# V asked for two batches at a time, fewer weight pieces with places of their own, and new places in the order of work

## The chip, the cores and the metric

One Trainium2 chip; the kernel runs on one of its cores. The metric is the device time of one execution in microseconds. Lower is better.

## The reference

Two stages. The first is causal attention with B = 8 batches, H = 8 heads, S = 576 positions, D = 64, and Nb = 16 beacon positions ahead of the keys that every query sees. The second is a soft mixture of experts over the N = 4608 tokens that come out, with E = 8 experts of 4 slots each, Dm = 512 and F = 1024. All inputs are float32.

```python
k_all = np.concatenate([beacon_k, k], axis=2); v_all = np.concatenate([beacon_v, v], axis=2)
scores = where(causal, -1e9, q @ k_all.T / sqrt(D))
a = softmax(scores);  x = (a @ v_all) as (B*S, H*D)
logits = x @ phi                                  # (N, 32)
d = softmax(logits, over tokens);  slot_input = d.T @ x
for e in range(E): slot_out[e] = relu(slot_input[e] @ w1[e]) @ w2[e]
out = softmax(logits, over slots) @ slot_out      # (4608, 512) float32
```

## The kernel before

**Steps.** The attention runs in 32 steps, one for each pair of heads; `n` is the step, `divmod(n, 4)` gives the batch `b` and the pair `g` in it. In a step the scores of pair `n` are made in four parts (letters `0` to `3`; each ends in an exponential on ScalarE, and part 1 is followed by two masking operations on GpSimd, L339), and the products with V of pair `n - 1` are made (`A` and `B`), then normalised on VectorE (`N`). Two pairs make a quad of q and of k; `T` and `U` transpose the next quad's halves. `x` takes one piece of the second stage's work on the previous batch from a list (`Q` fills it).

**Order.** The whole order of a step is a string of letters in the table `order`: the entry at minus `n` if there is one, else that of `n % 4`. All engines work through their own instructions in the order in which the letters issue them, so a letter's place decides what waits behind what on each engine.

**V.** V of one batch comes as two tiles of 128 partitions by 8 heads by two rows of 64 (`load_v`, tag `vf`, 512 KB a request, three buffers) and a tail of 80 rows (`load_tail`, tag `vl`). The letters a, b, e, f (first tile) and g, h, i, j (second tile) each cast a quarter of a tile from float32 to float16 into `vh[b % 2]`, on GpSimd or, for those in the string `dve`, on VectorE. `t` casts the tail, `c` and `d` load the beacons' V. At `g = 0` these letters mean the batch that just runs, else the next one, so `f` and `i` of a batch are done in its own first step.

**Requests on SyncE (SP).** V, tails, and q and k of the quads (`load_quad`, four requests of 288 KB, three buffers each) are requested from SP's queue, in the order in which `requests(n)` after each step writes them. SP goes through its queue on its own; a request whose buffer is still read waits there, and all behind it wait too.

**Weights.** The experts' weights are 32 pieces of 1 MB in float32, written as float16 by requests from GpSimd's queue (`load_w`). Letter `w` asks for pieces until `want(n)` are requested; in step 31 the rest is. 24 pieces have places of their own (12 tiles of 8 KB a partition in the pool `wh`, which the output tiles take over at the end); the last eight take buffers of V, q and k (`homes`). The last three pieces (`halved`) come in two halves of columns, all first halves ahead of all second halves.

**End.** After step 31 come the last routing pieces, `layer1` with ReLU, `turn` (transposes into `hTz`, a tile that GpSimd has to clear first, L654), `layer2` over the pieces in order, and the output rows, first for the left half of three groups, then their right half, then six whole groups of 1 MB.

Of the kernel before, what the change touches and what calls it, by code (L numbers as in the profile page):

```python
# [8 lines left out]
FP = mybir.dt.float32  # L9
F16 = mybir.dt.float16  # L10
# [7 lines left out]
def kernel(  # L18
# [22 lines left out]
    UL = U - 4 * P  # L41
# [12 lines left out]
    GB = H // 2  # L54
# [21 lines left out]
    qkp = ctx.enter_context(tc.tile_pool(name="qkp", bufs=3))  # L76
    vfp = ctx.enter_context(tc.tile_pool(name="vfp", bufs=3))
    vlp = ctx.enter_context(tc.tile_pool(name="vlp", bufs=2))
    exq = ctx.enter_context(tc.tile_pool(name="exq", bufs=2))
    sml = ctx.enter_context(tc.tile_pool(name="sml", bufs=4))  # L80
    NW = 24
    wh = ctx.enter_context(tc.tile_pool(name="wh", bufs=NW // 2))
    sc_scope = ExitStack()
    ps_sc = sc_scope.enter_context(tc.tile_pool(name="ps_sc", bufs=1, space=PSUM, side="right"))
# [3 lines left out]
    qf, kf = {}, {}  # L88
# [18 lines left out]
                    in_=src[b, h0:h0 + 2].rearrange("h s d -> (h s) d").rearrange(  # L107
                        "(p j) d -> p j d", j=J))

    vf = {}  # L110
    vten = v.tensor

    def vpairs(row, n, step, h0=0, nh=H):
        return bass.AP(vten, (row + h0 * S) * D, [[step * D, n], [S * D, nh], [1, step * D]])

    def load_v(b, what):
        base = b * H * S - Nb
        if what in (0, 1):
            t = vf[(b, what)] = vfp.tile([P, H, 2 * D], FP, name="vf", tag="vf")
            if what == 0 and b == 0:  # L120
                nc.vector.memset(t[0:Nb // 2, 0:1, :], 0.0)
                nc.sync.dma_start(out=t[Nb // 2:P, 0:1, :], in_=vpairs(base + Nb, P - Nb // 2, 2, 0, 1))
                nc.sync.dma_start(out=t[:, 1:H, :], in_=vpairs(base, P, 2, 1, H - 1))
            else:
                nc.sync.dma_start(out=t[:, :, :], in_=vpairs(base + 2 * P * what, P, 2))

    def load_tail(b):
        vf[(b, 2)] = vlp.tile([P, H, D], FP, name="vl", tag="vl")
        (nc.sync if b else nc.gpsimd).dma_start(
            out=vf[(b, 2)][0:UL], in_=vpairs(b * H * S - Nb + 4 * P, UL, 1))  # L130

    def put_t(b, eng):
        eng.tensor_copy(out=vh[b % 2][0:UL, 4, :, 0:D], in_=vf[(b, 2)][0:UL])

    def load_beac(b, r):
        nc.gpsimd.dma_start(out=vh[b % 2][64 * r:64 * r + Nb // 2, 0, :, 0:D],
# [1 line left out]

    NPC = 4 * E
    wv = {}  # L140
    homes = ["vf", "vf", "qf", "kf", "vf", "qf", "kf", "qf", "kf"][:NPC - NW]
    assert len(homes) == NPC - NW

    XH = 3
# [5 lines left out]
    def load_w(x):  # L150
        (e, r), hf = reqs[x]
        m = pieces.index((e, r))
        if (e, r) not in wv:
            if m < NW:
                if m % 2 == 0:
                    wv["pair"] = wh.tile([P, 4096], F16, name="w", tag="w")
                t = wv["pair"][:, 2048 * (m % 2):2048 * (m % 2) + 2048]
            else:
                tag = homes[m - NW]
                pool, cols = {"vf": (vfp, 2048), "qf": (qkp, 2304), "kf": (qkp, 2304)}[tag]  # L160
                t = pool.tile([P, cols], F16, name="wx", tag=tag)[:, 0:2048]
            wv[(e, r)] = t
        t = wv[(e, r)]
        if r < 2:
            src = moe_w1[e, r * 256:r * 256 + 256].rearrange("(s p) f -> p s f", p=P)
            t = t.rearrange("p (s f) -> p s f", s=2)
        else:
            src = moe_w2[e, (r - 2) * 512:(r - 1) * 512].rearrange("(p s) d -> p s d", p=P)
            if hf is None:
                src = src.rearrange("p s d -> p (s d)")  # L170
            else:
                src = src[:, :, 256 * hf:256 * hf + 256]
                t = t.rearrange("p (s d) -> p s d", s=4)[:, :, 256 * hf:256 * hf + 256]
        nc.gpsimd.dma_start(out=t, in_=src)  # L174
# [16 lines left out]
    bv0 = setup[0:Nb // 2, 1024:2048].rearrange("p (h x) -> p h x", h=H)  # L191
    nc.gpsimd.dma_start(out=bv0, in_=beacon_v[0].rearrange("h (n r) d -> n h (r d)", r=2))
    load_first(1)
    load_v(0, 0)
    load_v(0, 1)
    load_quad(1)
    load_quad(2)
    phif = const.tile([P, NDC, NSL], FP, name="phif")
# [29 lines left out]
    vh = [const.tile([P, NCH, H, DD], F16, name=f"vh{i}") for i in range(2)]  # L228
# [11 lines left out]
    hTz = const.tile([P, NFC, E * HY], F16, name="hTz")  # L240
# [31 lines left out]
    def beac(m):  # L272
        nc.gpsimd.tensor_copy(out=kT[m % 2][:, :, 0:Nb], in_=bkT[:, 2 * m:2 * m + 2, :])
# [111 lines left out]

    def put_v(b, R, z, r, eng):
        eng.tensor_copy(out=vh[b % 2][64 * r:64 * r + 64, 2 * R + z, :, 0:D],  # L387
                        in_=vf[(b, R)][64 * z:64 * z + 64, :, D * r:D * r + D])

    def put_b(r, eng):  # L390
        eng.tensor_copy(out=vh[0][64 * r:64 * r + Nb // 2, 0, :, 0:D],
# [125 lines left out]
    wl = 0  # L517

    def want(n):
        return int(0.64 * n) if n < 24 else int(15 + 2 * (n - 24))  # L520

    lastb = [lambda: xt_last(0, nc.vector), lambda: xt_last(1, nc.vector), lambda: sums(0, 6)]
    casts = {"a": (0, 0, 0), "b": (0, 0, 1), "e": (0, 1, 0), "f": (0, 1, 1),
             "g": (1, 0, 0), "h": (1, 1, 1), "i": (1, 0, 1), "j": (1, 1, 0)}
    dve = "fej"
    order = {0: "0Awf1xB2kNxi3TU", 1: "01QxbA2Ba3NTwU", 2: "0h1tAxckdx2BwxN3TU", 3: "01AjxBNg23eTwU",
             -2: "0ABwaT1ZV2NWiUbk3", -3: "01AcB2dN3weTU", -4: "0A1htBfgNj2kwp3TU", -5: "01baAwBNQ2x3TU",
             -29: "0QAB1N2xxx3w", -30: "0xABN1x2xw3L", -31: "0Ax1B2Nwxx3x"}

    def step(n, c):  # L530
        nonlocal wl
        b, g = divmod(n, GB)
        vb = b if g == 0 else b + 1
        if c in "0123":
            score(n, int(c))
        elif c == "A":
            for a in range(2):
                attend(n - 1, a, (0, 1, 2))
        elif c == "B":
            for a in range(2):  # L540
                attend(n - 1, a, (3, 4))
        elif c == "N":
            norm(n - 1)
        elif c == "x":
            if work:
                work.pop(0)()
        elif c == "Q":
            work.extend(routing(b - 1))
        elif c == "L":
            work.extend(lastb)  # L550
        elif c in "TUVW":
            m, w = (n // 2 + 1, 1) if n % 2 == 0 else ((n + 3) // 2, 0)
            if n == 1:
                m, w = 1, int(c in "VW")
            elif c in "VW":
                w = 0
            if m < NQ:
                transp(m, w, int(c in "UW"), n == 1 and c in "UW")
        elif c in "abefghij":
            if vb < B:  # L560
                put_v(vb, *casts[c], nc.vector if c in dve else nc.gpsimd)
        elif c in "cd":
            if vb < B:
                load_beac(vb, "cd".index(c))
        elif c == "t":
            if vb < B:
                put_t(vb, nc.vector if c in dve else nc.gpsimd)
        elif c == "Z":
            beacons()
        elif c == "p":  # L570
            nc.gpsimd.tensor_copy(out=phih[:, :, :, :],
                                  in_=phif[:, :, :].unsqueeze(2).broadcast_to([P, NDC, 4, NSL]))
        elif c == "k":
            if n // 2 + 1 < NQ:
                beac(n // 2 + 1)
        elif c == "w":
# [6 lines left out]
    def next_quad():  # L583
        if quads:
            load_quad(quads.pop(0))

    early = "0r1qq"
    reqs_at = {0: "1q", 1: "", 2: "r0q", 3: "", -2: "0r"}

    def requests(n):  # L590
        b, g = divmod(n, GB)
        for c in reqs_at.get(-n, reqs_at[g]):
            if c == "1" and b + 1 < B:
                load_v(b + 1, 1)
            elif c == "0" and b + 2 < B:
                load_v(b + 2, 0)
            elif c == "q":
                next_quad()
            elif c == "r" and b + 2 < B:
                load_tail(b + 2)  # L600

    score(0, 0)
    score(0, 1)
# [8 lines left out]
    for r in range(2):  # L612
# [4 lines left out]
        out=bkf[:, :, :],  # L617
        in_=beacon_k.rearrange("b h n d -> (b h n) d").rearrange("(p j) d -> p j d", j=8))
    nc.gpsimd.dma_start(out=phif[:, :, :], in_=moe_phi.rearrange("(c p) e -> p c e", p=P))
    score(0, 3)  # L620
    for c in early:
        if c in "01":
            load_v(1, int(c))
        elif c == "r":
            load_tail(1)
        else:
            next_quad()
    for x in range(4):
        score(1, x)
    for c in "TUABNVW":  # L630
        step(1, c)
# [19 lines left out]
    si_piece(B - 1)  # L651
    logit_piece(B - 1, 1)
    assert wl == len(reqs)
    nc.gpsimd.memset(hTz[:, :, :], 0.0)  # L654
# [135 lines left out]
```

## Time and profile before

| | |
|---|---|
| three runs | 206.95, 208.53, 209.72 us; median 208.53 |
| profiled execution | 206.11 us, of which the profile's span is 204.4 us |
| mean granted TensorE clock | 0.959 |
| busy: PE, VectorE, ScalarE, GpSimd | 157.4, 129.7, 131.3, 111.8 us |
| moved by DMA | 55.81 MB in 46217 packets, mean 273 GB/s |
| weights | 24 requests into own places, 11 into borrowed ones |
| V | 16 requests of about 512 KB, 8 tails of 160 KB |

Times are microseconds from the first instruction of the profiled execution. The three runs lie within 1.3% of one another. A busy share is an average over stages with different limits; DMA rates count the bytes as they are written, so a weight that is read as float32 and written as float16 counts half of what is read.

### The profile page before, as it was taken

How to read it: one execution, taken by the hardware profiler on the slowest of the kernel's cores; microseconds unless marked ns; L12 is line 12 of the kernel's file. 1: busy time of each engine (PE TensorE's matmuls, PEld its weight loads, DVE VectorE, ACT ScalarE, POOL GpSimd, SP SyncE). 2: the span in 40 equal slices, each digit the busy share in tenths (PEclk: the TensorE clock that was granted, in tenths of full speed). 3: DMA queues.
4: the chain of work that ended last, by engine and by line, in shares of the span. 5: the costliest groups of instructions: out<-in, count | busy, mean ns of one | idle time of the engine just before them, and what ended most of it. 6: DMA issues, size and time to landing. Idle time of an engine off the chain costs nothing.

```text
span 204.4 us, 7928 instructions
## 1 busy us (share of the span) xinstructions
PE 157.4 (77%) x3474; PEld 115.4 (56%) x3474; DVE 129.7 (63%) x270; ACT 131.3 (64%) x195; POOL 111.8 (55%) x194
## 2 busy tenths in 40 slices
PE   0777884999987889987879889899889867878300
PEld 0646662677765657765557667677668535643100
DVE  2594876578776777866686778679725320679500
ACT  2584787289876687876687778688685320389400
POOL 8394379757559657746853794899556341000000
PEclk9999999699999999999999999999999996999955
DMA  6999999998999999999999999999999999999996
GB/s 202 305 353 303 275 396 252 293 245 257 189 346 295 245 336 264 266 196 345 311 233 344 274 265 199 315 193 188 213 212 215 215 209 198 151 331 370 422 417 285
DMA packets 46217, 55.81 MB, mean 273 GB/s; under 512 B 8791, under 2 KB 31311, under 8 KB 45415
## 3 DMA queue, kind: packets, MB, share of 16 engines
q1 hardware_dynamic: 34391, 37.55, 57.6%
q0 software_dynamic: 11648, 17.46, 47.8%
q8 instruction: 27, 0.44, 0.8%
q10 hardware_dynamic: 144, 0.29, 0.5%
q14 instruction: 7, 0.06, 0.1%
HBM read 62.75 MB, written 9.44 MB: 353 GB/s over the span
## 4 chain that ended last, share of the span: by engine, by line
PE 35%; POOL 19%; DMA 12%; issue 12%; ACT 7%; DVE 6%; POOLq 1%; DVEq 0%; ACTq 0%
PE av L368 10%; PE sc L315 9%; POOL ex L339 8%; DMA wx<-in_moe_w_dram 7%; ACT ex L327 5%; PE tr L285 4%; POOL vh L387 4%; DVE osb L710 4%; POOL w L174 3%; DMA vh<-in_beacon_v_dram 3%; PE tr L410 3%; DMA setup<-in_beacon_k_dram 3%; PE av L691 2%; ACT osb L708 2%; PE tr L425 2%
## 5 line engine op out<-in xcount | busy, mean ns | idle before, releaser
L327 ACT ACTIVATE ex<-sc 128x1024 f16<-128x1024 f32 (+3 forms) x128 | 105.4, 869 | 33.7 <-PE sc L315 21.2
L339 POOL TENSOR_SCALAR_AFFINE_SELECT ex<-ex 64x512 f16<-64x512 f16 x64 | 40.6, 634 | 38.4 <-ACT ex L327 36.6
L315 PE MATMUL sc<-qT,kT 64*64 64x80 bf16 (+4 forms) x768 | 47.0, 304 | 6.3 <-ACT ex L327 3.7
L368 PE MATMUL av<-vh,ex 128*128 128x65 f16 x945 | 42.9, 199 | 6.0 <-DMA vh<-in_beacon_v_dram 2.8
L368 PEld LDWEIGHTS <-ex 128*128 128x128 f16 (+1 forms) x960 | 37.1, 107 | 15.8 <-issue 7.6
L315 PEld LDWEIGHTS <-kT 64*64 64x64 bf16 x768 | 20.8, 108 | 17.9 <-issue 9.9
L387 POOL CAST vh<-vf 64x512 f16<-64x512 f32 x37 | 23.4, 635 | 11.4 <-DMA vf<-in_v_dram 9.7
L382 DVE TENSOR_TENSOR xb<-av,r 128x640 f16<-128x640 f32 (+1 forms) x32 | 26.1, 814 | 1.1
L286 DVE COPY kT<-tr 128x640 bf16<-128x640 bf16 (+1 forms) x29 | 21.3, 773 | 4.7 <-PE tr L285 4.1
L286 DVE COPY qT<-tr 128x640 bf16<-128x640 bf16 (+1 forms) x29 | 21.3, 765 | 1.6 <-PE tr L285 1.4
L379 DVE RECIPROCAL r<-av 128x10 f32<-128x10 f32 (+1 forms) x32 | 7.0, 218 | 22.5 <-PE av L368 22.5
L708 ACT ACTIVATE osb<-fp,rc 128x256 f32<-128x256 f32 (+1 forms) x24 | 12.8, 578 | 11.6 <-PE fp L706 11.0
L174 POOL DMA_DIRECT2D w<-in_moe_w_dram x24 | 16.2, 677 | 0.0
L323 PE MATMUL sc<-mk,idb 64*64 64x128 bf16 x256 | 15.5, 223 | 0.6 <-issue 0.6
L387 DVE CAST vh<-vf 64x512 f16<-64x512 f32 x27 | 15.1, 558 | 0.7
L285 PE MATMUL tr<-idb,qf 128*64 128x128 bf16 x270 | 12.4, 235 | 3.7 <-issue 2.8
L710 DVE TENSOR_SCALAR osb<-fp,rc 128x256 f32<-128x256 f32 (+1 forms) x24 | 13.6, 614 | 2.0 <-PE fp L706 1.9
L706 PE MATMUL fp<-soh,eLh 128*128 128x256 f16 (+1 forms) x48 | 11.6, 324 | 3.1 <-ACT osb L708 1.5
L415 DVE COPY xT<-tr 128x1024 f16<-128x1024 f16 x14 | 9.6, 691 | 4.9 <-PE tr L410 4.4
L323 PEld LDWEIGHTS <-idb 64*64 64x64 bf16 x384 | 11.8, 111 | 0.8 <-issue 0.8
L285 PEld LDWEIGHTS <-qf 128*64 128x64 bf16 x270 | 9.3, 118 | 5.1 <-issue 2.9
L285 PE MATMUL tr<-idb,kf 128*64 128x128 bf16 x270 | 11.4, 223 | 0.0
(107 smaller groups left out, 173.8 us busy)
## 6 DMA issues: line engine op xcount, KB each, us to landing
w<-in_moe_w_dram POOLq DMA_DIRECT2D x24, 512.0 KB, 8.4
qf<-in_q_dram SPq DMA_DIRECT2D x32, 288.0 KB, 8.0
kf<-in_k_dram SPq DMA_DIRECT2D x31, 288.0 KB, 7.6
vf<-in_v_dram SPq DMA_DIRECT2D x15, 512.0 KB, 9.2
out_dram<-osb SPq DMA_DIRECT2D x6, 1024.0 KB, 8.5
wx<-in_moe_w_dram POOLq DMA_DIRECT2D x5, 512.0 KB, 13.5
wx<-in_moe_w_dram POOLq DMA_DIRECT2D x6, 256.0 KB, 15.2
out_dram<-osb SPq DMA_DIRECT2D x6, 256.0 KB, 3.3
```

Of the source, the lines that this page charges most:

```text
L174: nc.gpsimd.dma_start(out=t, in_=src)
L285: nc.tensor.transpose(tp[64 * x:64 * x + 64, j - j0, :], hi, idb[:, :])
L286: (nc.scalar.copy if act else nc.vector.tensor_copy)(out=dst[:, :, Nb:U].rearrange("p y (s j) -> p y s j", j=J)[:, :, :, j0:j1], in_=tp[:, ...
L315: nc.tensor.matmul(sc[64 * r:64 * r + 64, a, c:c + w], kt[64 * a:64 * a + 64, lhs], qt[64 * a:64 * a + 64, q0:q0 + w], start=True, stop=stop)
L323: nc.tensor.matmul(sc[64 * r:64 * r + 64, a, c:c + w], idb[h, h], m_[h, r, :], start=False, stop=True)
L327: nc.scalar.activation(e[:, o:o + 2 * pitch].rearrange("p (a t) -> p a t", a=2)[:, :, 0:w], sc[:, :, 0:w], AF.Exp, scale=scale)
L339: nc.gpsimd.affine_select(out=ap, in_=ap, compare_op=AL.is_ge, fill=0.0, base=-r, pattern=[[0, 4], [1, P]], channel_multiplier=-2)
L368: nc.tensor.matmul(avout(n, a, i), e[:, c:c + m], vh[b % 2][:, j, h, :], start=(j == 0), stop=(j == i))
L382: nc.vector.tensor_tensor(out=xo, in0=avv[:, :, :, 0:D], in1=r5[:, 0:w, :].unsqueeze(3).broadcast_to([P, w, NCH, D]), op=AL.mult)
L387: eng.tensor_copy(out=vh[b % 2][64 * r:64 * r + 64, 2 * R + z, :, 0:D], in_=vf[(b, R)][64 * z:64 * z + 64, :, D * r:D * r + D])
L708: nc.scalar.activation(osb[:, j, w], fp_[:, w], AF.Copy, scale=rc[:, i:i + 1])
L710: nc.vector.tensor_scalar(out=osb[:, j, w], in0=fp_[:, w], scalar1=rc[:, i:i + 1], scalar2=None, op0=AL.mult)
```

## The change

V of batches 0 and 1 is requested as before. For batches 2 to 7 one request brings one half (R = 0 or 1) of V of two batches, 1 MB, into a tile of 16 heads. The tag `vf` has three buffers still, now of 8 KB a partition. A buffer is free again when both batches are cast. The requests from SP stand in a new table by step, `reqs_at`, instead of a pattern by `g`.

Of the 32 weight pieces 20 have places of their own (10 tiles in `wh`), and 12 take buffers of V, q and k, two to a buffer of V. `want(n)` asks for 0.60 n instead of 0.64 n pieces up to step 23, and one piece fewer from step 24 on.

The letters of nearly all steps are laid out anew. The casts of a batch's V are now all in the three steps ahead of it. The clearing of `hTz` goes from the end to step 7 (letter `m`).

```diff
-    NW = 24
+    NW = 20
...
+    def vtile(b, R):
+        return (b, 0) if b < 2 else (b - b % 2, R)
+
+    def vslot(b, R):
+        return H * (R if b < 2 else b % 2)
+
+    def load_v(b, R):
+        row = b * H * S - Nb + 2 * P * R
+        if vtile(b, R) not in vf:
+            vf[vtile(b, R)] = vfp.tile([P, 2 * H, 2 * D], FP, name="vf", tag="vf")
+        t = vf[vtile(b, R)]
+        s0 = vslot(b, R)
...
+            nh = H if b < 2 else 2 * H
+            nc.sync.dma_start(out=t[:, s0:s0 + nh, :], in_=vpairs(row, P, 2, 0, nh))
...
-    homes = ["vf", "vf", "qf", "kf", "vf", "qf", "kf", "qf", "kf"][:NPC - NW]
+    homes = ["vf", "vf", "vf", "vf", "qf", "kf", "vf", "vf", "qf", "kf", "qf", "kf"][:NPC - NW]
...
-        return int(0.64 * n) if n < 24 else int(15 + 2 * (n - 24))
+        return int(0.60 * n) if n < 24 else int(14 + 2 * (n - 24))
...
-    order = {0: "0Awf1xB2kNxi3TU", 1: "01QxbA2Ba3NTwU", 2: "0h1tAxckdx2BwxN3TU", 3: "01AjxBNg23eTwU",
-             -2: "0ABwaT1ZV2NWiUbk3", -3: "01AcB2dN3weTU", -4: "0A1htBfgNj2kwp3TU", -5: "01baAwBNQ2x3TU",
-             -29: "0QAB1N2xxx3w", -30: "0xABN1x2xw3L", -31: "0Ax1B2Nwxx3x"}
+    order = {0: "0wA1xBN2kx3TU", 1: "0Q1xbA2wBaf3NTU", 2: "0e1tAxcdwx2BxN3TkU", 3: "01AjxBg2i3NhTUw",
+             -2: "0AwBaT1VZ2NWi3Ubk", -3: "01AcB2dN3weTU", -4: "0A1htBfgN2kwp3TUj", -5: "01AbwBNQaf2x3TU",
+             -7: "01AjxmBg2i3NhTUw", -29: "0QxAB1N2x3w", -30: "0xxABN1xw23L", -31: "0Ax1xx2BNwx3x"}
...
+        elif c == "m":
+            nc.gpsimd.memset(hTz[:, :, :], 0.0)
...
-    early = "0r1qq"
-    reqs_at = {0: "1q", 1: "", 2: "r0q", 3: "", -2: "0r"}
+    tails, vreqs = list(range(1, B)), [(b, R) for b in (1, 2, 4, 6) for R in range(2)]
+    early = "vvrqq"
+    reqs_at = {2: "vr", 3: "v", 4: "q", 5: "r", 6: "q", 8: "vq", 10: "rq", 12: "qv", 14: "vrq", 17: "q", 18: "rq", 21: "v", 22: "rqq", 24: "qq"}
...
-    nc.gpsimd.memset(hTz[:, :, :], 0.0)
```

In the new table `v` is the next V request, `q` the next quad, `r` the next tail.

More of the change, by code (lines that the diff above doesn't have):

```diff
@@ L108, in load_quad @@
                         "(p j) d -> p j d", j=J))
-    vf = {}
+    vf, vl = {}, {}
     vten = v.tensor
@@ L114, in vpairs @@
         return bass.AP(vten, (row + h0 * S) * D, [[step * D, n], [S * D, nh], [1, step * D]])
[L116 to L125, printed above, removed]
+    def vtile(b, R):
[8 more added lines that the diff above has]
+        s0 = vslot(b, R)
+        if b == 0 and R == 0:
+            nc.vector.memset(t[0:Nb // 2, 0:1, :], 0.0)
+            nc.sync.dma_start(out=t[Nb // 2:P, 0:1, :], in_=vpairs(row + Nb, P - Nb // 2, 2, 0, 1))
+            nc.sync.dma_start(out=t[:, 1:H, :], in_=vpairs(row, P, 2, 1, H - 1))
+        else:
+            nh = H if b < 2 else 2 * H
+            nc.sync.dma_start(out=t[:, s0:s0 + nh, :], in_=vpairs(row, P, 2, 0, nh))
     def load_tail(b):
-        vf[(b, 2)] = vlp.tile([P, H, D], FP, name="vl", tag="vl")
+        vl[b] = vlp.tile([P, H, D], FP, name="vl", tag="vl")
         (nc.sync if b else nc.gpsimd).dma_start(
-            out=vf[(b, 2)][0:UL], in_=vpairs(b * H * S - Nb + 4 * P, UL, 1))
+            out=vl[b][0:UL], in_=vpairs(b * H * S - Nb + 4 * P, UL, 1))
     def put_t(b, eng):
-        eng.tensor_copy(out=vh[b % 2][0:UL, 4, :, 0:D], in_=vf[(b, 2)][0:UL])
+        eng.tensor_copy(out=vh[b % 2][0:UL, 4, :, 0:D], in_=vl[b][0:UL])
     def load_beac(b, r):
@@ L159, in load_w @@
                 tag = homes[m - NW]
-                pool, cols = {"vf": (vfp, 2048), "qf": (qkp, 2304), "kf": (qkp, 2304)}[tag]
-                t = pool.tile([P, cols], F16, name="wx", tag=tag)[:, 0:2048]
+                if tag == "vf":
+                    if "vf" not in wv:
+                        wv["vf"] = vfp.tile([P, 4096], F16, name="wx", tag=tag)
+                        t = wv["vf"][:, 0:2048]
+                    else:
+                        t = wv.pop("vf")[:, 2048:4096]
+                else:
+                    t = qkp.tile([P, 2304], F16, name="wx", tag=tag)[:, 0:2048]
             wv[(e, r)] = t
@@ L193 @@
     load_first(1)
-    load_v(0, 0)
-    load_v(0, 1)
+    for R in range(2):
+        load_v(0, R)
     load_quad(1)
@@ L387, in put_v @@
         eng.tensor_copy(out=vh[b % 2][64 * r:64 * r + 64, 2 * R + z, :, 0:D],
-                        in_=vf[(b, R)][64 * z:64 * z + 64, :, D * r:D * r + D])
+                        in_=vf[vtile(b, R)][64 * z:64 * z + 64, vslot(b, R):vslot(b, R) + H,
+                                            D * r:D * r + D])
     def put_b(r, eng):
@@ L585, in next_quad, with request @@
             load_quad(quads.pop(0))
-    early = "0r1qq"
-    reqs_at = {0: "1q", 1: "", 2: "r0q", 3: "", -2: "0r"}
-    def requests(n):
[L591 to L600, printed above, removed]
+    tails, vreqs = list(range(1, B)), [(b, R) for b in (1, 2, 4, 6) for R in range(2)]
+    early = "vvrqq"
+    reqs_at = {2: "vr", 3: "v", 4: "q", 5: "r", 6: "q", 8: "vq", 10: "rq", 12: "qv", 14: "vrq", 17: "q", 18: "rq", 21: "v", 22: "rqq", 24: "qq"}
+    def request(c):
+        if c == "v" and vreqs:
+            load_v(*vreqs.pop(0))
+        elif c == "q":
+            next_quad()
+        elif c == "r" and tails:
+            load_tail(tails.pop(0))
+    def requests(n):
+        for c in reqs_at.get(n, ""):
+            request(c)
     score(0, 0)
@@ L621 @@
     for c in early:
[L622 to L627, printed above, removed]
+        request(c)
     for x in range(4):
```

## The prediction

> **What bounds the kernel now.** I read the page first: engine shares, the slices, the DMA part and the chain.
>
> ```profile
> span 204.4 us, 7928 instructions
> PE 157.4 (77%) x3474; PEld 115.4 (56%) x3474; DVE 129.7 (63%) x270; ACT 131.3 (64%) x195; POOL 111.8 (55%) x194
> PE   0777884999987889987879889899889867878300
> DMA  6999999998999999999999999999999999999996
> ...
> HBM read 62.75 MB, written 9.44 MB: 353 GB/s over the span
> PE 35%; POOL 19%; DMA 12%; issue 12%; ACT 7%; DVE 6%; POOLq 1%; DVEq 0%; ACTq 0%
> ```
>
> No engine is full, the chain wanders over all of them, but the DMA row is at 9 almost from end to end. So the second view is that row by stages (columns: busy time and count of PE, PEld, DVE, ACT and POOL, then clock, DMA share, GB/s written). [...]
>
> ```profile
> 2.50:20.00 17.50, 11.48 (x232) 8.84 (x233) 10.66 (x25) 9.14 (x14) 11.32 (x21) 1.00 1.10 328
> 20.00:47.50 27.50, 22.71 (x535) 16.84 (x531) 18.94 (x32) 19.68 (x27) 17.32 (x31) 0.94 1.13 297
> 47.50:50.00 2.50, 2.18 (x53) 1.55 (x46) 2.47 (x4) 2.32 (x5) 2.37 (x4) 1.00 0.85 273
> 50.00:52.50 2.50, 2.50 (x84) 2.18 (x84) 2.19 (x8) 2.24 (x4) 2.20 (x5) 1.00 0.70 91
> 52.50:85.00 32.50, 28.58 (x697) 21.60 (x692) 24.05 (x45) 25.12 (x38) 21.41 (x38) 1.00 1.12 287
> 85.00:87.50 2.50, 2.11 (x59) 1.65 (x57) 2.42 (x8) 2.24 (x3) 2.09 (x4) 1.00 0.91 198
> 87.50:130.00 42.50, 35.96 (x894) 27.43 (x895) 30.36 (x59) 31.68 (x46) 26.87 (x47) 1.00 1.12 278
> 130.00:132.50 2.50, 2.39 (x64) 1.82 (x63) 1.83 (x3) 1.39 (x2) 2.41 (x5) 1.00 0.96 306
> 132.50:175.00 42.50, 36.49 (x823) 27.11 (x815) 21.42 (x54) 22.89 (x39) 24.08 (x39) 0.96 1.11 204
> 177.50:180.00 2.50, 2.10 (x20) 1.09 (x19) 2.12 (x5) 2.07 (x6) 0.00 (x0) 1.00 0.72 216
> 180.00:204.40 24.40, 9.32 (x36) 3.94 (x35) 10.91 (x18) 10.56 (x19) 0.00 (x0) 0.80 0.95 367
> ```
>
> From 2.5 us on the DMA engines are full at about 1.12, with dips at 47.5 to 52.5, 85 to 87.5, 130 to 132.5 and 177.5 to 180. Taken against 1.12 the first four dip rows miss 0.6, 0.9, 0.5 and 0.4 us, 2.4 us in all; the one at 177.5, against 1.0 for a single queue of stores, misses 0.7. From 132.5 on only weights move: 204 GB/s written as f16 is 408 read as f32, so a piece (1 MB read) costs an estimated 2.5 us of all DMA engines. The same bytes move after the change as before. **The kernel is bound by the amount of DMA work, and an edit can win little more than those 3.1 us of idle DMA time.**
>
> The end is read next: the last weights, the PE that waits for them, the stores.
>
> ```profile
> L174 POOL DMA_DIRECT2D wx<-in_moe_w_dram x1: 742/742/742, 159.5 to 159.5; - x1
> DMA to landing us min/median/max: 16.0/16.0/16.0
> ...
> 167.61 2.02 POOL L654 MEMSET hTz<- 128x2304 f16 x1
> 169.66 0.29 DVE L684 COPY hTz<-tr 128x64 f16<-128x64 f16 x2 [2.52 <-POOL hTz L654]
> 169.91 2.98 PE L691 MATMUL av<-w,hTz 128*32 128x256 f16 x64 [3.01 <-DVE hTz L684]
> ...
> 174.28 1.60 PE L691 MATMUL av<-wx,hTz 128*32 128x256 f16 x52
> ...
> L759 SPq DMA_DIRECT2D out_dram<-osb x6: 332/336/571, 185.3 to 192.1; - x6
> DMA to landing us min/median/max: 5.7/8.5/11.3
> ```
>
> The last first-half weight is asked for at 159.5 and lands 16.0 later, at 175.5; PE ends the products that need it at 174.28 + 1.60 = 175.9. So PE's 3 us behind the hTz memset were nearly free: the weight came only then. The last six stores land between 185.3 + 5.7 = 191.0 and 192.1 + 11.3 = 203.4, one MB every 2.5 us, with their data ready long before. The end is thus the landing of the weights plus a fixed tail of stores.
>
> **The change part by part.** The sum is made against the span of 204.4 us; that run took 206.11 us in all and the median of the runs shown is 208.53, so I add the difference to the median.
>
> *V by two batches, tiles of 8 KB.* Before, SP stands in front of a V request until a cast frees the tile, and q and k queue behind it:
>
> ```profile
> SPq L125 <- DVE vh L387: 32.6, 6, 8.6
> L125 SPq EVENT_SEMAPHORE  x1: 6707/6707/6707, 44.0 to 44.0; - x1
> ...
> L125 SPq EVENT_SEMAPHORE  x1: 8561/8561/8561, 115.1 to 115.1; - x1
> ...
> POOL vh L387 <- DMA vf<-in_v_dram: 9.7, 4, 3.6
> ```
>
> SP is stuck from 44.0 to 50.7, which is the dip at 47.5 to 52.5. After the change the request for batches 4 and 5 waits for a tile of batch 1, whose last cast is at the end of step 4, and quad 7 follows as soon as its own buffers are free. I expect the two dips of 47.5 to 52.5 filled and that of 85 in part: of 2.0 us I take 1.5 (bounds 0 and 2.4). Six requests fewer save their fixed costs. Four q and k requests of 288 KB, issued 124.1 to 126.1, land 7.3 to 7.6 later, so one per 0.7 us or some 400 GB/s, as the 1 MB stores do; a request that stands in a queue costs at most 0.05 us beside its bytes, so 0.1 (bounds 0 and 0.3).
>
> ```profile
> L105 SPq DMA_DIRECT2D qf<-in_q_dram x2: 602/688/775, 124.1 to 124.8; - x2
> L105 SPq DMA_DIRECT2D kf<-in_k_dram x2: 401/514/627, 125.6 to 126.1; - x2
> ...
> DMA to landing us min/median/max: 7.3/7.4/7.6
> ```
>
> [...]
>
> *V in time.* Each V request is 0.5 MB longer, 1.9 us at the loop's 280 to 297 GB/s. The tightest is the second half of V of batches 2 and 3: it can be asked for only after cast f in step 4, as V of batch 2 is now, at 30.5, when that lands 6.7 later, at 37.2. With its own extra 0.5 MB and that of the request ahead it should land at 41 to 44. The casts of step 7 want it at about 48 (POOL's first select of step 7 is followed by a cast at 48.69). That covers it by 4 us; without the cover POOL's selects, casts and weight requests queue behind it.
>
> ```profile
> L125 SPq DMA_DIRECT2D vf<-in_v_dram x1: 378/378/378, 30.5 to 30.5; - x1
> ...
> DMA to landing us min/median/max: 6.7/6.7/6.7
> ...
> 48.69 0.69 POOL L387 CAST vh<-vf 64x512 f16<-64x512 f32 x1
> ```
>
> *Casts of V moved* (e, f, h, i, j and g now all in the three steps ahead of the batch): the same number, 0.43 us on DVE or 0.61 on POOL each, but POOL no longer waits for V in the middle of the loop:
>
> ```profile
> 60.02 0.61 POOL L387 CAST vh<-vf 64x512 f16<-64x512 f32 x1 [2.22 <-DMA vf<-in_v_dram]
> ...
> 95.53 0.61 POOL L387 CAST vh<-vf 64x512 f16<-64x512 f32 x1 [1.43 <-DMA vf<-in_v_dram]
> ```
>
> These 3.65 us go. They count at the end only as far as an earlier weight request finds DMA idle, so 1.0 of them (bounds 0 and 2.6).
>
> *20 own places, and the pace of the requests.* By step 24 the new rule has asked for 14 pieces and the old for 15; with the last V no longer stuck until 123.6, q and k of the last quad come some 8 us earlier. So before the pair of requests of step 25 DMA has one piece less to do, 2.5 us. That pair stands seventh of 15 letters instead of thirteenth; a step is 4.5 us (98 exps from 41.0 to 149.9, four a step), so it comes 1.8 us earlier. Net loss 0.7 (bounds -0.5 and 2.5). From there on two pieces a step need 5.0 us of DMA against 4.5, so the queue stays full to the end. The twelve borrowed places are free before they are wanted (the last V cast is in step 27, the last quad's transposes in step 28, their pieces are asked for in step 31): 0.
>
> ```profile
> L327 ACT ACTIVATE ex<-sc x98: 508/968/1024, 41.0 to 149.9; 128x1024 f16<-128x1024 f32 x25, 128x928 f16<-128x928 f32 x25, 128x992 f16<-128x992 f32 x24, 128x416 f16<-128x416 f32 x24
> ```
>
> *The memset of hTz in step 7.* PE gains up to 2.5 us at 167 but then waits for the weight of 175.5: 0.3 (bounds 0 and 0.4). In step 7 its 2.0 us sit between POOL's selects and its casts; step 8 has no casts, so I charge 0.3 (bounds 0 and 2.0).
>
> Sum: -1.5 - 0.1 - 1.0 + 0.7 - 0.3 + 0.3 = -1.9. Span 202.5, median **206.6 us**; with each of the likelier bounds 205.0 to 209.0.
>
> **The rivals.** A difference of 2%, 4.2 us, is about what a measurement of this kernel can tell from no change.
>
> *Much faster.* All idle DMA time goes (3.1 us) and V moves better in the larger requests. If the 7 MB of V that are asked for by pairs went at the 328 GB/s of 2.5 to 20 us instead of 278, they would take 3.8 us less: 208.5 - 3.1 - 2.2 (that part of 3.8 which is not already in filled dips) = 203.2. For it: V and the wait on it show as the disorder of the loop. Against it: the packets stay 512 bytes, and a full DMA row leaves little.
>
> *A price on each request.* A store of 1 MB issued at 185.3 lands 5.7 later, 3.2 more than its 2.5 us of bytes. If such a fixed part held the DMA engines, six requests fewer would save up to 19 us and give 189. The rows of q and k above, 0.7 us apart, speak against it. [...]
>
> *Slower: DMA runs dry ahead of step 25.* Everything of V, q and k is moved earlier and weights are asked for later, and weight requests are tied to steps. If the loop from step 6 to 25 (19 steps of 4.5 us) becomes 3% slower by the new order of letters, 2.6 us, with the full 2.5 us of the missing piece and the 2.0 of the memset in step 7, and the dips give back 1.5, the weights land 5.6 us later: 214.1. It decides as soon as the DMA share around 110 to 130 us falls under 0.9 for over 4 us. For it: 1.12 there today hangs on V and q, k that come late; against it: POOL loses waits rather than gaining them.
>
> *Nothing.* V's waits go but another wait of the loop takes their place and DMA has no more or less idle time: 208.5.
>
> **How the numbers follow.** Likeliest, 206.6: 0.42. Nothing, or a small loss: 0.12. Both lie within 2%: 0.54. Much faster 0.24, a price on each request 0.02, so 0.26 for faster by over 2%; slower 0.20. The range has to reach to both outer cases: 202.8, just past the faster one's 203.2, to 211.2, half way into the slower one.
>
> **What would show it.** Right: no wait of POOL casts on V after 30 us; DMA share at 1.1 through 47 to 53; the last first-half weight lands 1 to 3 us earlier and the stores' tail stays at 25 us or so; the wait of hTz is gone and PE waits for a weight in its place. The step that I am least sure of is the share at 110 to 132: a dip of 2 us is allowed for, one of 5 makes me wrong on the slow side. I am wrong on the fast side if the loads themselves show higher GB/s at a full share.

## The result and the profile after

| | median us (lowest to highest) | ratio to before, 95% interval |
|---|---|---|
| before | 208.06 (205.95 to 211.40), 20 runs | 1 |
| changed | 210.77 (208.88 to 213.22), 20 runs | **1.0157 [1.0123, 1.0192]** |

The change makes the kernel slower by 1.6%, 2.7 us; 206.6, a gain of 1.9, was forecast. Medians are over all runs, ratios over the runs within 1.5% of the fastest of their kernel, to which the first profiled execution of the changed kernel (213.09 us) does not belong. So the lines below are of a second profile of the same kernel, a1_after_again, beside a second one of the kernel before, d1_before_again (span 205.6 us; the 204.4 us shown above are among its fastest). The old kernel timed against itself gave 0.9949 [0.9915, 0.9982]: two kernels less than some 0.6% apart are not told apart here, whatever their interval.

The page of a1_after_again (engine shares, the slices, the packets):

```profile
span 209.9 us, 7920 instructions
PE 161.1 (77%) x3474; PEld 117.2 (56%) x3474; DVE 129.5 (62%) x270; ACT 131.5 (63%) x195; POOL 111.9 (53%) x194
DMA  6999999999999999999999979399999999989996
DMA packets 36905, 55.81 MB, mean 266 GB/s; under 512 B 8695, under 2 KB 18927, under 8 KB 36103
q1 hardware_dynamic: 25079, 37.55, 55.2%
```

The engines have the same work as before. What is new is in the DMA row: a 7, 9, 3 in slices 24 to 26, at 121 to 136 us, where before had nines. The stages show it (busy time and count of PE, PEld, DVE, ACT, POOL; clock; DMA share; GB/s written). a1_after_again:

```profile
20.00:47.50 27.50, 21.60 (x488) 16.26 (x485) 17.94 (x31) 17.84 (x24) 15.98 (x28) 0.88 1.10 291
47.50:52.50 5.00, 4.68 (x120) 3.76 (x120) 3.51 (x9) 4.82 (x8) 4.09 (x6) 1.00 1.09 306
52.50:85.00 32.50, 28.32 (x665) 21.11 (x666) 23.68 (x44) 23.14 (x34) 22.22 (x38) 0.95 1.08 289
85.00:115.00 30.00, 25.27 (x644) 19.66 (x642) 21.01 (x42) 22.84 (x33) 18.78 (x33) 1.00 1.10 286
115.00:120.00 5.00, 4.14 (x101) 3.15 (x100) 4.05 (x8) 3.42 (x5) 2.69 (x5) 1.00 1.05 294
120.00:125.00 5.00, 4.68 (x121) 3.53 (x118) 4.28 (x8) 4.37 (x10) 4.56 (x9) 1.00 0.67 172
125.00:130.00 5.00, 4.84 (x122) 3.64 (x122) 3.69 (x10) 4.04 (x6) 3.96 (x7) 1.00 0.95 144
130.00:135.00 5.00, 4.98 (x135) 3.94 (x131) 4.45 (x9) 4.47 (x6) 3.38 (x6) 1.00 0.43 71
...
140.00:175.00 35.00, 30.12 (x696) 22.58 (x690) 16.57 (x45) 18.50 (x31) 18.28 (x31) 1.00 1.06 207
```

The same stages of d1_before_again:

```profile
20.00:47.50 27.50, 22.80 (x539) 16.91 (x534) 18.44 (x32) 19.71 (x27) 17.52 (x31) 0.94 1.13 299
47.50:52.50 5.00, 4.67 (x134) 3.74 (x127) 4.66 (x11) 4.55 (x8) 4.58 (x8) 1.00 0.79 178
52.50:85.00 32.50, 26.70 (x659) 20.36 (x654) 22.09 (x42) 23.22 (x35) 19.35 (x35) 1.00 1.12 288
85.00:115.00 30.00, 25.64 (x621) 19.45 (x611) 22.36 (x43) 21.86 (x32) 19.64 (x34) 0.94 1.02 254
115.00:120.00 5.00, 5.00 (x116) 3.49 (x113) 3.51 (x7) 3.70 (x7) 3.48 (x6) 1.00 1.17 268
120.00:125.00 5.00, 4.62 (x117) 3.50 (x114) 4.15 (x9) 4.71 (x8) 4.19 (x8) 1.00 1.12 296
125.00:130.00 5.00, 4.40 (x125) 3.50 (x126) 3.89 (x10) 3.56 (x5) 2.09 (x4) 1.00 1.11 233
130.00:135.00 5.00, 3.70 (x100) 2.83 (x93) 2.82 (x6) 2.98 (x5) 4.27 (x7) 1.00 0.93 293
```

The dip at 47.5 to 52.5 is filled, as forecast: 0.79 to 1.09, 1.5 us of DMA work. Between 85 and 115 the share is 1.10 against 1.02, another 2.4 us. But from 115 to 135 it is 1.05, 0.67, 0.95, 0.43 against 1.17, 1.12, 1.11, 0.93: differences of 0.12, 0.45, 0.16 and 0.50 times 5 us, 6.2 us. From 140 us on only weights are in flight, and the share is 1.06, so a share a little over 1 is not idle time; the two stretches at 0.67 and 0.43 alone make 4.8 us of the difference. **The idle time of the DMA engines was moved, not removed.** Counted in bytes (GB/s times us of these rows, 20 to 135 us) 30.9 MB are written against 31.5. The 0.6 MB that are missing are about one weight piece, which is 0.5 MB as it is written; the rest of the dip is work that was done earlier. In 130 to 135 they write 71 GB/s instead of 293: V, q and k have all arrived, and weights are not yet asked for. SP's last k request, a1_after_again and then d1_before_again (durations in ns, then first to last start):

```profile
L105 SPq DMA_DIRECT2D kf<-in_k_dram x6: 327/402/428, 105.6 to 121.7; - x6
```

```profile
L105 SPq DMA_DIRECT2D kf<-in_k_dram x8: 400/430/1527, 99.9 to 128.2; - x8
```

It goes out 6.5 us earlier. What is left to do then waits for step 25. Its pair of weight requests, the last weight request, and the time from that to landing, a1_after_again:

```profile
L189 POOL DMA_DIRECT2D w<-in_moe_w_dram x2: 703/705/707, 133.4 to 134.1; - x2
...
L189 POOL DMA_DIRECT2D wx<-in_moe_w_dram x1: 740/740/740, 171.2 to 171.2; - x1
DMA to landing us min/median/max: 12.6/12.6/12.6
```

The same of d1_before_again:

```profile
L174 POOL DMA_DIRECT2D w<-in_moe_w_dram x2: 582/644/706, 133.1 to 133.8; - x2
...
L174 POOL DMA_DIRECT2D wx<-in_moe_w_dram x1: 750/750/750, 167.6 to 167.6; - x1
DMA to landing us min/median/max: 12.7/12.7/12.7
```

The pair goes out at nearly the same time, 133.4 against 133.1, with 18 pieces left to ask for instead of 17; the last weight lands at 171.2 + 12.6 = 183.8 against 180.3, and the run ends 26.1 against 25.3 later. So of the 4.3 us between these two spans 0.3 come ahead of the pair, 3.2 between the pair and the last weight, 0.8 behind.

At the end PE waits for weights one after another (start, busy time, operation, idle time before it and what ended that). PE in a1_after_again, and then the last such wait in d1_before_again:

```profile
175.88 0.41 PE L704 MATMUL av<-wx,hTz 128*32 128x256 f16 x8 [1.66 <-DMA wx<-in_moe_w_dram]
177.20 0.29 PE L704 MATMUL av<-wx,hTz 128*32 128x256 f16 x4 [0.91 <-DMA wx<-in_moe_w_dram]
178.54 0.30 PE L704 MATMUL av<-wx,hTz 128*32 128x256 f16 x4 [1.05 <-DMA wx<-in_moe_w_dram]
179.93 0.40 PE L704 MATMUL av<-wx,hTz 128*32 128x256 f16 x4 [1.08 <-DMA wx<-in_moe_w_dram]
```

```profile
176.30 0.29 PE L691 MATMUL av<-wx,hTz 128*32 128x256 f16 x4 [0.46 <-DMA wx<-in_moe_w_dram]
```

The last first-half weight comes at 179.9 instead of 176.3, 3.6 us later, where 1 to 3 earlier was forecast.

### The profile page after: what moved, and what is told of

The parts are those of the page before. It is cut to its first block, busy times and chain, and to the rows that moved or that the text cites. A ratio compares the mean times of both kernels' runs of the same rounds, so it can differ in the third digit from the quotient of the medians.

```text
span 211.4 us, 7920 instructions
## 1 busy us (share of the span) xinstructions
PE 161.8 (77%) x3474; PEld 118.0 (56%) x3474; DVE 130.2 (62%) x270; ACT 131.2 (62%) x195; POOL 111.8 (53%) x194
## 3 DMA queue, kind: packets, MB, share of 16 engines
q1 hardware_dynamic: 25079, 37.55, 55.2%
## 4 chain that ended last, share of the span: by engine, by line
PE 39%; DMA 18%; ACT 12%; POOL 10%; issue 9%; DVE 6%; DVEq 0%; ACTq 0%; POOLq 0%
DMA wx<-in_moe_w_dram 12%; PE sc L330 11%; PE av L383 11%; ACT ex L342 9%; PE tr L300 6%; POOL ex L354 4%; DMA vh<-in_beacon_v_dram 4%; DVE osb L723 3%; PE tr L426 3%; DMA setup<-in_beacon_k_dram 3%; PE tr L464 2%; POOL w L189 2%; DVE kT L301 2%; ACT osb L721 1%; PE sc L338 1%
## 5 line engine op out<-in xcount | busy, mean ns | idle before, releaser
L342 ACT ACTIVATE ex<-sc 128x1024 f16<-128x1024 f32 (+3 forms) x128 | 105.5, 869 | 38.3 <-PE sc L330 22.4
L354 POOL TENSOR_SCALAR_AFFINE_SELECT ex<-ex 64x512 f16<-64x512 f16 x64 | 40.6, 635 | 46.7 <-ACT ex L342 44.5
L330 PE MATMUL sc<-qT,kT 64*64 64x80 bf16 (+4 forms) x768 | 48.9, 310 | 9.0 <-ACT ex L342 5.7
L383 PE MATMUL av<-vh,ex 128*128 128x65 f16 x945 | 43.7, 202 | 5.7 <-DMA vh<-in_beacon_v_dram 4.2
L383 PEld LDWEIGHTS <-ex 128*128 128x128 f16 (+1 forms) x960 | 38.2, 109 | 14.8 <-POOL ex L354 6.5
L330 PEld LDWEIGHTS <-kT 64*64 64x64 bf16 x768 | 21.8, 110 | 21.9 <-issue 13.8
L402 POOL CAST vh<-vf 64x512 f16<-64x512 f32 x37 | 22.7, 615 | 7.4 <-DMA vf<-in_v_dram 5.7
L719 PE MATMUL fp<-soh,eLh 128*128 128x256 f16 (+1 forms) x48 | 12.5, 354 | 2.7 <-ACT osb L721 1.2
L189 POOL DMA_DIRECT2D w<-in_moe_w_dram x20 | 13.8, 693 | 0.0
L189 POOL DMA_DIRECT2D wx<-in_moe_w_dram x15 | 9.3, 625 | 5.9 <-DMA wx<-in_moe_w_dram 5.9
L426 PE MATMUL tr<-idh,xb 128*128 128x128 f16 (+1 forms) x140 | 11.3, 232 | 1.0 <-DVE kT L301 1.0
```

Source lines behind the costliest of these rows:

```text
L330: nc.tensor.matmul(sc[64 * r:64 * r + 64, a, c:c + w], kt[64 * a:64 * a + 64, lhs], qt[64 * a:64 * a + 64, q0:q0 + w], start=True, stop=stop)
L342: nc.scalar.activation(e[:, o:o + 2 * pitch].rearrange("p (a t) -> p a t", a=2)[:, :, 0:w], sc[:, :, 0:w], AF.Exp, scale=scale)
L354: nc.gpsimd.affine_select(out=ap, in_=ap, compare_op=AL.is_ge, fill=0.0, base=-r, pattern=[[0, 4], [1, P]], channel_multiplier=-2)
L383: nc.tensor.matmul(avout(n, a, i), e[:, c:c + m], vh[b % 2][:, j, h, :], start=(j == 0), stop=(j == i))
L426: nc.tensor.transpose(tp[:, ii, t, 0:m], xb[b % 2][0:m, i, 2 * t:2 * t + 2, :].rearrange("p h d -> p (h d)"), idh[0:m, 0:m])
```

## The experiments

Each run is 6 to 12 executions beside the kernel before on the same chip; brackets hold the 95% interval of the ratio.

**First: is it the missing piece or a late loop?** a1_after_again is the changed kernel with no edit.

> The changed kernel once more, for a second profile. Theory 1 (dry DMA: all of V, q and k is asked for early and the weights by steps, so the DMA engines run out of work ahead of step 25): ratio 1.012 to 1.020, and again 4 us or more of missing DMA time between 115 and 140 us. Theory 2 (late loop: PE is held up in steps 5, 8 and 21, by the beacon request behind longer V requests and by stalls named issue): the same ratio, but step 25 starts 4 us or more later than before and the dry stretch is only its consequence. If a profile shows the loop on time and DMA dry, theory 2 falls; if it shows the loop late, theory 1 alone isn't enough.

Measured: 210.49 us, 1.0172 [1.0117, 1.0227]. The loss is repeated. The trace, shown above, has the pair of step 25 on time and DMA dry ahead of it, so theory 2 falls.

a2_after_pace64, the changed kernel with the old pace:

```diff
-        return int(0.60 * n) if n < 24 else int(14 + 2 * (n - 24))
+        return int(0.64 * n) if n < 24 else int(15 + 2 * (n - 24))
```

> The changed kernel with the old pace of weight requests (0.64 n, then 15 + 2(n - 24)). Theory 1: one piece of 2.5 us more is moved ahead of step 25, so 1.5 to 2.5 us come back: ratio to before 1.003 to 1.008. Theory 2: the loop is as late as in the changed kernel; the piece helps as much only if the weights still set the end; ratio 1.005 to 1.016.

Measured: 209.01 us, 1.0041 [0.9994, 1.0088]. This one line takes away 1.2 of the 1.6%, as theory 1 said. But the dip is still there: the DMA share over 115 to 135 us is 0.89, against 0.78 in a1_after_again and 1.09 in d1_before_again. So it is the missing piece that costs time, and not the dip by itself.

a3_after_pace75, the same line with `0.75 * n` and `18 + 2 * (n - 24)`:

> The changed kernel with a faster pace of weight requests (0.75 n up to step 23, then 18 + 2(n - 24)): four pieces, 10 us of DMA work, are moved ahead of step 25, so DMA can't run dry there. Theory 1: all the missing DMA time comes back, ratio 0.985 to 1.000. Theory 2: the weights land earlier but the loop ends as late, PE sets the end; ratio 1.005 to 1.015, with PE no longer waiting for a weight at the end.

Measured: 209.98 us, 1.0076 [1.0022, 1.0131]; more weight ahead of step 25 brings nothing further, as theory 2 said. PE in its trace:

```profile
177.98 1.60 PE L704 MATMUL av<-wx,hTz 128*32 128x256 f16 x52
```

All 52 products run without a wait for a weight. That alone holds for the kernel before, too (its row at 174.28). The difference is in the products of the last second halves: in a3 the last of these weights lands at 176.7 and the products start only at 182.9, in before it lands at 179.5 and they start at 179.2. Here PE sets the end, not DMA.

a4_before_pace60, the kernel before with the new pace and nothing else (the first diff the other way):

> The kernel before with the new, slower pace (0.60 n, then 14 + 2(n - 24)) and nothing else. Theory 1: its V, q and k still come late and fill the gap, so only part of the 2.5 us is lost: ratio 1.002 to 1.010, with a wider dip of the DMA share at 130. Theory 2: the loop is as in the kernel before, so ratio 1.000 to 1.004.

Measured: 210.16 us, 1.0124 [1.0065, 1.0184]. So the pace alone costs the old kernel what the whole change costs, within the intervals, and more than either theory allowed. Its DMA share over 115 to 135 us is 1.07, so it loses as much without a dry stretch there. Its trace has 18 pieces left at the pair, too, and the last weight at 170.7 + 12.7 = 183.4:

```profile
L174 POOL DMA_DIRECT2D w<-in_moe_w_dram x2: 703/705/707, 134.2 to 134.9; - x2
...
L174 POOL DMA_DIRECT2D wx<-in_moe_w_dram x1: 740/740/740, 170.7 to 170.7; - x1
DMA to landing us min/median/max: 12.7/12.7/12.7
```

**Second: the other parts alone.** c1_before_new_order, the kernel before with the new table of letters (and with it the clearing of `hTz` in step 7):

```diff
-    order = {0: "0Awf1xB2kNxi3TU", ...}
+    order = {0: "0wA1xBN2kx3TU", ...}
-    nc.gpsimd.memset(hTz[:, :, :], 0.0)
```

> The kernel before with the new letters of all steps, the clearing of hTz in step 7 with them, but its own loads, its 24 places and its pace. Theory P (the slower pace is the whole loss, the loads and the letters are nothing beside it): ratio 0.996 to 1.004. Theory R (the new letters make the loop late): 1.004 to 1.012, step 25 starting 2 us or more later than in a kernel with the old letters.

Measured: 208.15 us, 1.0038 [0.9999, 1.0078]. No effect that can be told apart; the pair of step 25 goes out at 133.2.

c2_loads_alone, the changed kernel with the old letters, the old pace and the clearing at the end, so that only V by two batches, the 20 places and the table of requests are left of the change:

```diff
-    order = {0: "0wA1xBN2kx3TU", ...}
+    order = {0: "0Awf1xB2kNxi3TU", ...}
```

> The new loads alone: V by two batches in 1 MB requests, three tiles of 8 KB, 20 places, the new table of requests; but the old letters, the old pace and the clearing of hTz at the end. Theory P: 0.996 to 1.004. Theory Q (a 1 MB request makes what stands behind it late, and moving V, q and k early leaves DMA dry later): 1.004 to 1.010, with 3 us or more of missing DMA time between 115 and 145 us as in the changed kernel with the old pace.

Measured: 210.28 us, 1.0141 [1.0081, 1.0201], above both forecasts, though with the new letters the same loads at the same pace stand at 1.0041 (a2). One stage of its trace:

```profile
85.00:115.00 30.00, 26.91 (x645) 20.67 (x642) 22.74 (x45) 22.52 (x33) 18.31 (x32) 0.94 0.88 212
```

The DMA share is 0.88 over 30 us. The old letters cast f and i of a batch in its own first step, so they hold the larger tiles longer, which fits a late next request; the experiment doesn't separate that from the loop, which is late as well. What follows is only that the new loads are likely slower with the old letters than with the new (the two intervals just overlap).

c3_after_pace64_halfreq, a2 with each 1 MB request made as two of 512 KB into the same tile:

```diff
-            nc.sync.dma_start(out=t[:, s0:s0 + nh, :], in_=vpairs(row, P, 2, 0, nh))
+            for h in range(0, nh, H):
+                nc.sync.dma_start(out=t[:, s0 + h:s0 + h + H, :], in_=vpairs(row, P, 2, h, H))
```

> The changed kernel at the old pace, with each 1 MB request of V asked for as two of 512 KB, one right behind the other, into the same tile at the same place of the queue. Theory P: the size of a request costs and brings nothing, so ratio 1.000 to 1.008, as the changed kernel at the old pace had (1.004). Theory Q: the smaller requests let others through, ratio 0.996 to 1.001. [...]

Measured: 208.48 us, 1.0086 [1.0040, 1.0131], against 1.0041 for a2; the intervals overlap. The likeliest price of six more requests is 0.45%, less than can be told apart; a price of 3.2 us each, as the rival in the prediction had it, an estimated 9% in all, is ruled out.

c4_before_clear7, the kernel before with `hTz` cleared in step 7:

```diff
+             -7: "01AjxmBNg23eTwU",
-    nc.gpsimd.memset(hTz[:, :, :], 0.0)
```

> The kernel before with only the clearing of hTz moved to step 7. The prediction charged 0.3 us and credited 0.3: ratio 0.997 to 1.003; DVE no longer waits for it, and PE waits for a weight in its place. If instead PE's 3 us were on the path, 0.988.

Measured: 208.68 us, 1.0041 [0.9996, 1.0087]. Neither a gain nor a loss.

**Third: the loop's start.** In step 5 PE stands behind a beacon load that is asked for from 29.0 us on and lands up to 7.5 us later. PE in before and in a1_after_again:

```profile
36.16 1.15 PE L368 MATMUL av<-vh,ex 128*128 128x65 f16 x30 [2.82 <-DMA vh<-in_beacon_v_dram]
```

```profile
37.24 1.92 PE L383 MATMUL av<-vh,ex 128*128 128x65 f16 x30 [3.90 <-DMA vh<-in_beacon_v_dram]
```

d1_before_again is the kernel before with no edit.

> The kernel before, unchanged, for a second profile and for the size of chance: ratio 0.996 to 1.004. Theory S (the arrival at step 25 sets the end: the last weight lands 47 to 49 us after the pair of requests in step 25 when 17 pieces are left by then, 49 to 51 when 18 are, and the end comes 25 us later): whatever the span of this execution, these two distances hold, and its step 25 starts between 126 and 130. Theory W (the amount of DMA work sets the end): the missing DMA time before 145 us stays near 2.4 us, wherever step 25 starts.

Measured: 206.71 us, 0.9949 [0.9915, 0.9982]: the size of chance, as said above. Both distances of theory S hold in its trace, 47.2 and 25.3 us. The missing DMA time doesn't stay near 2.4 us, as theory W had it: against 1.12 it is some 4 us in the rows 47.5 to 52.5 and 85 to 115 alone.

d2_before_early_beacons, the kernel before with the beacon loads in step 2 instead of 3, and `b` ahead of them:

```diff
-             -2: "0ABwaT1ZV2NWiUbk3", -3: "01AcB2dN3weTU",
+             -2: "0ABwabT1cdZV2NWiUk3", -3: "01AB2N3weTU",
```

> The kernel before with the beacons' V of batch 1 asked for in step 2 instead of step 3 (cast b goes ahead of them, as they overwrite part of what it writes), which takes away PE's wait of 2.8 us in step 5. Theory S: step 6 starts 1.5 to 2.8 us earlier and so does the pair of step 25, ratio 0.987 to 0.994. Theory W: the loop has no idle DMA time to win, ratio 0.996 to 1.003.

Measured: 206.10 us, 0.9945 [0.9908, 0.9982], the same as with no edit. In its trace step 6 starts at 38.3 instead of 41.0 (d1), but the pair of step 25 goes out no earlier, at 135.1. The wait of step 5 wasn't what set the old kernel's end.

d3_after_early_beacons, the same letters moved in the changed kernel:

> The changed kernel with the beacons of batch 1 asked for in step 2, which takes away PE's wait of 4 us in step 5. Theory S: 2 to 4 us come back in full, since DMA is dry for 6 us ahead of step 25: ratio to before 0.998 to 1.007 instead of 1.016. Theory W: the wait was covered, 1.012 to 1.018.

Measured: 208.79 us, 1.0092 [1.0050, 1.0134], against 1.0157 and 1.0172 without; the intervals overlap a little, so a gain of some 0.7% is likely and not shown; it lies between the two forecasts. In its trace step 6 starts at 38.8 instead of 42.8 and the pair of step 25 at 131.6 instead of 133.4: of a lead of 4.0 us 1.8 are left by then.

d4_after_pace64_early_beacons, d3 with the old pace:

> The changed kernel with the old pace of weight requests and the early beacons. Theory S: both gains add, 1.004 less 1.0 to 1.9%: ratio 0.985 to 0.995, faster than both kernels. Theory W: 1.000 to 1.006, as with the old pace alone.

Measured: 208.47 us, 1.0043 [1.0011, 1.0075], the same as a2 and as theory W said. Once the pace is the old one, the beacons bring nothing.

**Fourth: the pace by itself.** e1_before_pace68, the kernel before with `0.68 * n` and `16 + 2 * (n - 24)`:

> The kernel before with a faster pace (0.68 n, then 16 + 2(n - 24)): 16 pieces left behind the pair of step 25 instead of 17. Theory S (the end is the pair of step 25, plus 2.5 us a piece that is left, plus 31 us): the last weight lands 44 to 46.5 us after the pair; ratio 0.985 to 0.994 as long as the loop arrives as before. Theory L (more weight traffic in the loop makes its loads and PE's instructions late, so the loop gives the gain back): ratio 0.997 to 1.004, the pair of step 25 1.5 us or more later than 133.

Measured: 207.36 us, 0.9908 [0.9863, 0.9953], as theory S said.

e2_before_pace72, with `0.72 * n` and `17 + 2 * (n - 24)`:

> The kernel before with a still faster pace (0.72 n, then 17 + 2(n - 24)): 15 pieces left. Theory S alone: another 2.5 us, ratio 0.975 to 0.985, until PE sets the end: the loop's end plus 19 us to the first store, as the pace of 0.75 showed, so not under 0.98. Theory L: 1.000 to 1.010.

Measured: 206.06 us, 0.9892 [0.9853, 0.9931]. It is faster than both kernels by its interval, by 1.1% than before; beside the 0.9949 of no edit 0.6% are left, with intervals that overlap. Its PE:

```profile
173.61 1.60 PE L691 MATMUL av<-wx,hTz 128*32 128x256 f16 x52
```

One wait of 0.40 us for a weight is left ahead of them, at 170.6; the last weight lands at 176.2, and the products of the last second halves start only at 178.6. So PE sets the end here, too, and a higher pace has little more to give.

e3_after_pace68, the changed kernel with `0.68 * n` and `16 + 2 * (n - 24)`:

> The changed kernel with 0.68 n, then 16 + 2(n - 24): between the old pace (ratio 1.004) and 0.75 n (1.008). Theory S: 0.992 to 0.999. Theory L: 1.002 to 1.010.

Measured: 208.33 us, 0.9932 [0.9890, 0.9975]. With two constants altered the changed kernel isn't slower than before.

All together, by the number of pieces not yet asked for ahead of the pair of step 25 (ratios to before):

| pieces left | old kernel | changed kernel |
|---|---|---|
| 18 | 1.0124 (a4) | 1.0157, 1.0172 (as it is, a1) |
| 17 | 1, 0.9949 (as it is, d1) | 1.0041 (a2) |
| 16 | 0.9908 (e1) | 0.9932 (e3) |
| 15 | 0.9892 (e2) | |
| 14 | | 1.0076 (a3) |

From 18 to 17 the changed kernel gains 1.2%, 2.4 us, and from 17 to 16 1.1%, 2.3 us; in the old kernel the same steps are 1.2 and 0.9%. With the 0.6% that can't be told apart, this is the 2.5 us of DMA for a piece, until PE sets the end. Along a row the changed kernel is 0.2 to 0.9% above the old one: all the rest of the change is worth nothing, or a small loss.

The traces say the same from inside (us; a subtraction of the two times before it stands in "pair to last"):

| | pieces left | pair of step 25 | last weight landed | pair to last | from there to the end |
|---|---|---|---|---|---|
| before | 17 | 130.8 | 179.5 | 48.7 | 24.9 |
| d1 | 17 | 133.1 | 180.3 | 47.2 | 25.3 |
| a2 | 17 | 131.6 | 179.3 | 47.7 | 25.4 |
| c1 | 17 | 133.2 | 180.9 | 47.7 | 25.1 |
| c2 | 17 | 135.9 | 183.9 | 48.0 | 25.3 |
| c4 | 17 | 133.6 | 180.3 | 46.7 | 25.9 |
| d4 | 17 | 132.6 | 181.2 | 48.6 | 25.7 |
| a1 | 18 | 133.4 | 183.8 | 50.4 | 26.1 |
| a4 | 18 | 134.2 | 183.4 | 49.2 | 25.3 |
| d3 | 18 | 131.6 | 181.8 | 50.2 | 25.9 |
| e1 | 16 | 134.1 | 180.4 | 46.3 | 25.1 |
| e2 | 15 | 134.1 | 176.2 | 42.1 | 27.8 |
| a3 | 14 | 134.7 | 176.7 | 42.0 | 31.5 |

The last weight comes 46.7 to 48.7 us after the pair with 17 pieces left and 49.2 to 50.4 with 18, and the end 25 to 26 after that, until with 15 or 14 left PE sets it. So a run's end is when step 25 comes, plus what is left then. In this table the pair itself comes at 130.8 to 134.2 with the old loads and at 131.6 to 134.7 with the new loads and letters: the change doesn't make the loop later by more than one execution differs from another.

## Why the prediction was wrong

What bounds the kernel was right: DMA work up to the last weight, then a fixed tail (25.3 and 26.1 us). What failed is the sum over it, at two steps. The pace was put at a loss of 0.7 us and cost 2.4 (1.2%, a2 against the kernel as it is). All other terms together were put at a gain of 2.6 us, and a2, which has them all at the old pace, shows none: 1.0041, a loss of 0.9 us (interval -0.1 to 1.8).

**The pace of the requests** was the term that failed most. Its bound of 2.5 us is close to the measured 2.4, but 0.7 was taken, because the pair stands earlier among the letters of step 25 (eighth of 15, before thirteenth of 14) and was to go out 1.8 us sooner. A letter's place in the string is not its time on its engine. POOL at step 25 in before, and then in a1_after_again:

```profile
128.26 1.31 POOL L339 TENSOR_SCALAR_AFFINE_SELECT ex<-ex 64x512 f16<-64x512 f16 x2 [1.77 <-ACT ex L327]
129.63 1.26 POOL L387 CAST vh<-vf 64x512 f16<-64x512 f32 x2
130.84 1.28 POOL L174 DMA_DIRECT2D w<-in_moe_w_dram  x2
```

```profile
131.44 1.32 POOL L354 TENSOR_SCALAR_AFFINE_SELECT ex<-ex 64x512 f16<-64x512 f16 x2 [2.17 <-ACT ex L342]
132.83 0.61 POOL L402 CAST vh<-vf 64x512 f16<-64x512 f32 x1
133.38 1.40 POOL L189 DMA_DIRECT2D w<-in_moe_w_dram  x2
```

In both the pair stands behind two selects, which wait for ScalarE, and one or two casts. It comes 2.6 us behind the start of the selects before and 1.9 after: one cast, 0.6 us, is what the move gains. And the 8 us by which q and k were to come sooner (6.5 measured) were read as relief ahead of the pair. In fact they leave DMA with little to do: 4.8 us less DMA time in the two dry stretches, where the prediction allowed for 2 ("a dip of 2 us is allowed for, one of 5 makes me wrong on the slow side").

**The dips, 1.5 us.** They were filled (1.10 over 47.5 to 52.5 us in a2), and a2 shows no gain. The mistake is one of kind: the hole was filled with work that in the old kernel fills a later stretch, and no other requests took its place there, since the weights were tied to steps (share 0.45 in 130 to 135 us of a2, 0.93 in d1_before_again).

**V's waits, 1.0 us.** They went as forecast. From the view of waits of a1_after_again (us in total, times, longest):

```profile
PE av L704 <- DMA wx<-in_moe_w_dram: 4.7, 4, 1.7
...
POOL vh L402 <- DMA vf<-in_v_dram: 4.1, 2, 3.5
```

9.7 us in four became 4.1 in two, both ahead of 27 us. But the pair of step 25 goes out at 133.4 against 133.1: other waits of the loop took the place, POOL's for ScalarE among them, 42.1 us in all against 37.3 in d1_before_again.

**The requests' price.** Forecast 0.1; c3 agrees as far as it can tell. c3 lies 0.5 us under a2 in the median and 0.9 us over it by the ratio. The 3.2 us by which a store's landing exceeds its bytes in before (185.3 to 191.0, less 2.5), charged to the DMA engines for each request, would make c3's six further requests cost an estimated 19 us, which c3 doesn't show.

**V in time, and free places** were right: no POOL wait on V after 27 us, and the weight requests wait only for earlier weights (6.9 us in four in a1_after_again), not for a reader of V, q or k. The first two pieces in borrowed places are asked for in step 28 already (`want(28)` is 22), at 144.1 us, not in step 31.

**The clearing of `hTz`** was right: 0.3 gained and 0.3 charged, and c4 shows no difference; the wait is gone and PE waits for the weight in its place (the four rows of PE above, 4.7 us).

**The rivals.** What came is "DMA runs dry ahead of step 25". Its point of decision, a share under 0.9 for over 4 us, was passed (0.67 and 0.43, each over 5 us), but its 5.6 us were too many: the loop isn't 2.6 us late but 0.3, and c4 shows no cost of the memset. The missing piece remains. In "Much faster" the line that packets stay 512 bytes was wrong. In d1_before_again the queue of V, q, k and the stores had, in packets, MB and share:

```profile
q1 hardware_dynamic: 34391, 37.55, 56.9%
```

9312 packets fewer for the same 37.55 MB, and 55.2% of 209.9 us is 115.9 against 117.0: 1.1 us. The larger packets may have moved V a little cheaper; no gain of it is left at the end.

## What to carry to other kernels

Here several streams share full DMA queues (a share of 1.13 and 1.12 in 20 to 47.5 and 52.5 to 85 us of d1_before_again). Moving some of them earlier filled one stretch (0.79 to 1.09 in 47.5 to 52.5 us) and emptied another (0.93 to 0.43 in 130 to 135 us, 0.45 with the old pace), and gained nothing (1.0041 with the old pace), since no other was asked for in the place that they left. Look at who may issue requests in the stretch that becomes empty, and at what program step they hang. Count what is still to be asked for at the point from which the queue stays full, and price each piece in DMA time: here one line, 0.60 n and 14 instead of 0.64 n and 15, outweighed everything else that was laid out anew. And read a letter's place from the engine's own timeline: POOL waited 1.77 us before and 2.17 us after for ScalarE, and issued the pair of step 25 only behind the selects and casts that followed.

## What was not expected of the hardware

PE's granted clock falls to half around waits of 2.82 and 3.90 us inside the loop. In before it is 1.00 in 36 to 37.24 us, as the wait of 2.82 us for the beacons ends, 0.50 in 38 to 40 and 1.00 again in 41 to 47.5. The 0.88 of a1_after_again in 20 to 47.5 us, taken as stretches at half speed, is 2 x 0.12 x 27.5 = 6.6 us around its wait of 3.90 us; a part of them lies inside the wait, where they cost nothing: the 30 products right behind it take 1.92 us already, against 1.15 in before. The 0.94 of before is 3.3 us, all after its wait. With 0.95 in the next stage a1_after_again has some 10 us at half clock in the loop, d1_before_again (0.94 in 20 to 47.5 and in 85 to 115) some 7. How much of the small loss that is left at equal pace comes from the clock was not separated.
